# One kernel, four moves: block products in one run with a PSUM tile per bank, weight sums on VectorE, PSUM reads by halves, v over GpSimd's queue

## The chip, the cores and the metric

The kernel runs on one core of a Trainium2 chip. The metric is the device time of one execution in microseconds (us). Three timed runs of the kernel before gave 946.34, 945.3 and 944.76 us, a median of 945.3 us. The profiled execution took 946.52 us; its span, from the first instruction of the program to the last, is 944.7 us.

## What is computed

Attention within chunks of 64 positions (8 batches, 8 heads, 576 positions, head size 64), and then a feed-forward layer with a squared ReLU on the 4608 rows of 512 that it leaves:

```python
scores = scale * np.matmul(q_c, k_c.transpose(0, 1, 2, 4, 3))      # per chunk of 64
scores = scores - np.max(scores, axis=-1, keepdims=True)
attn = np.exp(scores)
attn = attn / (np.sum(attn, axis=-1, keepdims=True) + 1e-09)
out = np.matmul(attn, v_c)
x = out.transpose(0, 2, 1, 3).reshape(B * S, H * D)                # 4608 x 512
h = x @ w_in                                                       # 512 x 2048
g = np.maximum(h, 0.0) ** 2
y = (g @ w_out).astype(np.float32)                                 # 2048 x 512
```

The weights come as float64. Every matrix product of the feed-forward layer is made of three float32r products of a high and a low part (high times high, high times low, low times high).

## The kernel before

Rows are worked on in pairs of chunks, 128 rows each, 36 pairs in all. They form seven blocks: three of 4 pairs ("plain" blocks, numbered 0 to 2) and four of 6 pairs ("mixed" blocks, 3 to 6). The 2048 hidden columns are 16 slices of 128.

In a plain block one slice is 12 matmuls into the bank `h` (L602) and, two slices later, 12 matmuls into four output banks `o` (L638). ReLU, square and the split into high and low part lie between, on ScalarE (ACT) and VectorE (DVE). Block 0 runs beside the conversion of the weights.

In a mixed block two slices are made at once from 7 block products instead of 8, in the manner of Strassen and Winograd. One step is a pair of slices; there are 8 steps in a block and 32 in all. A step has 7 products of 6 matmuls each (L689, 384 columns; P0 to P6 in the order of `WAYS`) and 12 output groups of 3 matmuls each (L721, 512 columns), which multiply the squared columns of the step before by `w_out`. Products go into the one PSUM tile `both` of two banks, side 0 (A) or side 1 (C). P2 and what follows on side 0 adds up on P0, which ACT has first copied aside (`keep`, L695, tile `aside`); DVE adds side 1 and such a copy into `gf` (`add`, L698); the last part goes through ACT's ReLU (`positive`, L701). Then come the square (L704), the high part (ACT, L707) and the low part (DVE, L711). In the order of the work the outputs are spread between the products: the numbers of output groups after P0 to P6 are 0, 1, 0, 1, 2, 0, 0, then 3, then an attention clump, then the rest.

The left factors of the products are sums of blocks of `w_in`. They are made once, during blocks 1 and 2, by GpSimd (POOL): for each of 8 pairs of slices 16 elementwise instructions of 128 by 256 (L749 to L773), a rounding by ACT (L769, tile `combo`, one buffer), and a store of each result to DRAM (L776). The mixed steps fetch them again through a ring of 10 slots (L679). The scratch tile `temp` of the sums lies in the same place as `gf1`, where the first mixed step puts `kept(1)`; the ring, the split right factors `xc` and `gs_f` lie in the places of `w_in` slices, which the sums read. The right factors are built at the start of each mixed block (`build`, L1209, L1211, L1216) from the block's attention output, the tile `aside`.

Attention for pairs 8 to 35 goes in "clumps" between matmuls of the feed-forward layer. A clump is the value products of one pair (`values`, L342, 32 small matmuls) and the scores of the next (`scores`, L296, 32 small matmuls). Both use `both`: scores columns 0 to 255 of either bank, values columns 256 to 511. After the values ACT copies the result out of PSUM (`place`, L353); after the scores DVE reads them twice (`top`, L302; `less`, L306). The softmax, two transposes on DVE and a copy of the transposed probabilities on POOL (`keep_p`, L331), with four small DMAs on SP's queue, make the left factor of the next values. q, k and v come over SP's queue (L240, L270).

The order of the instructions on each engine is written out by a planner (class `Plan`). It has a cost for each operation, names for what is read and written, a rank (lower goes first), a gate, and a slack for attention's matmuls; it emits the instructions in the order of its own clock. The waits on the chip are not the planner's. They follow from which tiles an instruction reads and writes. For the planner the names "A" and "C" stand for the two banks; `scores` and `values` both write them, so that scores come after values by at least the slack of 0.5 us:

```python
entry = min(
    (x for x in ready[e] if max(x[0], free[e]) <= soonest + (hold if x[1] < self.RUSH else 0.0)),
    key=lambda x: (x[1], max(x[0], free[e]), x[2]),
)
```

Of the kernel before, what the change touches and what calls it, by code (L numbers as in the profile page):

```python
# [20 lines left out]
def kernel(  # L21
# [72 lines left out]
    both = psum["at"].tile([P, 2, DM], F32, name="both", tag="both")  # L94
    four = both.rearrange("p c (w h j) -> p c w h j", w=2, j=CH)
# [26 lines left out]
    wi = [None] * NF  # L122
    wo = [None] * NF
# [22 lines left out]
    def convert_w(n):  # L146
# [36 lines left out]
        def high():  # L183
            w = const.tile([P, 2, DM], F32R, name=f"w{kind}{f}", tag=f"w{n}")
            st["w"] = w
            nc.scalar.copy(w[:, 0], st["a"].bitcast(F32))  # L186
            hl = (w[:, 0], w[:, 1])
            if kind == "i":
                wi[f] = tuple(x.rearrange("p (c n) -> p c n", c=NCC) for x in hl)
            else:  # L190
                wo[f] = hl
# [70 lines left out]
    def load_v(pair):  # L262
# [3 lines left out]
        for c in range(2):  # L266
            bb, n0 = divmod(2 * pair + c, NCH)
            for b, r in enumerate(halves):
                s = v[bb, b * HH:(b + 1) * HH, n0 * CH:(n0 + 1) * CH, :]
                nc.sync.dma_start(out=t[r, c], in_=s.rearrange("h j d -> j h d"))  # L270
        return t

    class Quad:
# [19 lines left out]
        def scores(self):  # L293
            for a, t, c, b in itertools.product(range(2), repeat=4):
                h, own, to = 4 * b + 2 * a + t, halves[c], halves[b]
                nc.tensor.matmul(  # L296
                    four[to, c, 0, 2 * a + t], self.t["q"][own, h], self.t["k"][own, h], start=True, stop=True
                )

        def top(self):  # L300
            self.m = att.tile([P, 2, HH, 1], F32, name=f"m{self.pair}", tag="nm", bufs=2)
            nc.vector.tensor_reduce(self.m, four[:, :, 0], axis=AX.X, op=ALU.max)  # L302

        def less(self):
            self.e = late["pool"].tile([P, HH, 2, CH], F32, name=f"e{self.pair}", tag="e")
            nc.vector.tensor_tensor(  # L306
                self.e.rearrange("p h c j -> p c h j"), four[:, :, 0], self.m.broadcast_to([P, 2, HH, CH]),
                op=ALU.subtract,
            )
# [29 lines left out]
        def values(self):  # L339
            for a, c, b, t in itertools.product(range(2), repeat=4):  # L340
                own, to = halves[b], halves[t]
                nc.tensor.matmul(  # L342
                    four[to, b, 1, 2 * a + c], self.v[own, c, 2 * a + t],
# [3 lines left out]
        def place(self, part):  # L347
            j = self.pair - first_pair[self.b]
            got = four[:, :, 1].rearrange("p b (a c) i -> p b a (c i)", c=2)
            if self.b >= NCB:  # L350
                i = j % TH
                to = stage()[:, j // TH, :, i * P:(i + 1) * P].rearrange("p (b a) i -> p b a i", b=2)
                nc.scalar.copy(to, got)  # L353
                return
            xh, xl = (
                x[:, :, j * P:(j + 1) * P].rearrange("p (b a) i -> p b a i", b=2) for x in x_of(self.b)
            )
            if part == 0:
                nc.scalar.copy(xh, got)
            else:  # L360
                nc.vector.tensor_tensor(xl, got, xh.bitcast(F32), op=ALU.subtract)
# [10 lines left out]
    def bank(which, shape, name):  # L372
        kind, n = which
        if kind == "at":
            names = "abcdef"[:len(shape) - 1]
            t = both[:, n, :math.prod(shape[1:])]
# [179 lines left out]
    PARTS = [(q, m) for q in ("b11", "b21", "t1", "t2", "t3", "t4", "b22") for m in range(2)]  # L556
# [12 lines left out]
    def quarter(q):  # L569
# [5 lines left out]
        ("s3", "t3", 0), ("a22", "t4", 0), ("s4", "b22", 1),  # L575
# [94 lines left out]
    class Mixed(Step):  # L670
# [12 lines left out]
        def product(self, i):  # L683
# [3 lines left out]
            for c, u in some:  # L687
                l, r = ((0, 0), (0, 1), (1, 0))[u]
                nc.tensor.matmul(  # L689
                    both[:, side, :HN], w[:, l, c], part(x, r)[:, c], skip_group_check=True,  # L690
# [3 lines left out]
        def keep(self, i):  # L694
            nc.scalar.copy(snap(i), both[:, 0, :HN])  # L695

        def add(self, i, h, s):
            nc.vector.tensor_tensor(kept(i)[:, h * HN:(h + 1) * HN], both[:, 1, :HN], snap(s), op=ALU.add)  # L698

        def positive(self):  # L700
            nc.scalar.activation(kept(1)[:, :HN], both[:, 0, :HN], AF.Relu)  # L701
# [27 lines left out]
    class Combos:  # L729
# [17 lines left out]
        def both_of(self, to, x, y, op):  # L747
            for m in range(2):
                nc.gpsimd.tensor_tensor(self.temp(to + m)[:, 0], self.half(x)[m], self.half(y)[m], op=op)  # L749

        def join(self, to):
            nc.gpsimd.tensor_tensor(
# [3 lines left out]
        def less(self, to, i, x):  # L756
            t = self.temp(i)[:, 0]
            for y in self.half(x):
                nc.gpsimd.tensor_tensor(self.temp(to)[:, 0], t, y, op=ALU.subtract)
                t = self.temp(to)[:, 0]  # L760

        def from_it(self, i, x):
            t = self.temp(i)[:, 0]
            h, l = self.half(x)
            nc.gpsimd.tensor_tensor(t, h, t, op=ALU.subtract)
            nc.gpsimd.tensor_tensor(t, t, l, op=ALU.add)
# [644 lines left out]
```

## Time and profile before

| | |
|---|---|
| median of 3 runs | 945.3 us |
| profiled execution, its own time | 946.52 us |
| its span | 944.7 us |
| PE (matmul) busy | 884.2 us, 94% |
| PEld (weight load) busy | 727.6 us, 77% |
| DVE busy | 523.1 us, 55% |
| ACT busy | 344.6 us, 36% |
| POOL busy | 277.9 us, 29% |

PE's matmuls are pipelined and their ends are modelled, so that a busy PE is not PE at its peak; starts of weight loads (PEld) show its pace better. The number in brackets behind a row of the timeline is the idle time of that engine before the row, and what ended it. An engine other than PE that waits costs nothing as long as PE does not wait for it.

### The profile page before, as it was taken

The numbers are of one execution on the slowest core, as the hardware profiler recorded it, in microseconds if no ns is written. First come the engines' busy times: TensorE is split into PE (matmuls) and PEld (weight loads), VectorE is DVE, ScalarE is ACT, GpSimd is POOL, SyncE is SP. The second block draws the span as 40 slices with busy tenths as digits, with TensorE's granted clock in tenths as the row PEclk, the third lists the DMA queues.
The fourth block names the chain that finished last, engine by engine and source line by source line (L and its number), as shares of the span: only waits on it lengthen the run. The fifth ranks groups of instructions, "written<-read, shape, count | busy, mean of one in ns | idle before, by whom it ended". The sixth has DMA issues, their size and how long they took to land.

```text
span 944.7 us, 16464 instructions
## 1 busy us (share of the span) xinstructions
PE 884.2 (94%) x6142; PEld 727.6 (77%) x6142; DVE 523.1 (55%) x822; ACT 344.6 (36%) x597; POOL 277.9 (29%) x460
## 2 busy tenths in 40 slices
PE   9999999999999853999999999999999999999998
PEld 7787788878888643887778778777787888788886
DVE  6999984334467652445655554566455456332322
ACT  5888864443333322222233322223322224222222
POOL 2000012677667664221222222222212221222200
PEclk9999999999999975999999999999999999999999
DMA  7883534556955452666684677665767642744411
GB/s 193 265 245 112 191 63 111 129 124 151 241 124 127 107 139 68 176 150 143 133 165 129 163 157 155 143 135 116 206 131 155 138 107 78 201 101 113 121 45 68
DMA packets 268384, 132.72 MB, mean 140 GB/s; under 512 B 214416, under 2 KB 229008, under 8 KB 268304
## 3 DMA queue, kind: packets, MB, share of 16 engines
q0 software_dynamic: 43776, 73.42, 30.3%
q1 hardware_dynamic: 222272, 57.59, 27.6%
q8 instruction: 49, 0.80, 0.3%
q10 hardware_dynamic: 2256, 0.66, 0.3%
q14 instruction: 31, 0.25, 0.1%
HBM read 103.81 MB, written 24.12 MB: 135 GB/s over the span
## 4 chain that ended last, share of the span: by engine, by line
PE 54%; DVE 3%; POOL 2%; issue 2%; DMA 2%; ACT 2%; SPq 1%; DVEq 0%; POOLq 0%; ACTq 0%
PE o L721 26%; PE both L689 25%; DVE gf L698 2%; PE both L342 1%; PE both L296 1%; ACT aside L695 1%; DMA combos<-combo 1%; SPq L240 1%; POOL temp L749 1%; POOL combo L773 1%; DMA p<-et 0%; PE o L638 0%; ACT xc L1209 0%; DVE xc L1211 0%; POOL combos L776 0%
## 5 line engine op out<-in xcount | busy, mean ns | idle before, releaser
L689 PE MATMUL both<-xc,ring 128*128 128x384 f32 x1344 | 275.3, 349 | 48.3 <-DVE gf L698 20.2
L689 PEld LDWEIGHTS both<-xc,ring 128*128 128x128 f32 x1344 | 233.6, 191 | 88.9 <-DVE gf L698 39.6
L679 POOL DMA_DIRECT2D ring<-combos x224 | 118.6, 530 | 399.4 <-PE both L689 390.0
L721 PE MATMUL o<-wo,gs_f 128*128 128x512 f32 x576 | 151.9, 393 | 0.0
L721 PE MATMUL o<-wo,gs_s 128*128 128x512 f32 x576 | 148.2, 398 | 0.0
L602 PE MATMUL h<-x,wi 128*128 128x512 f32 x576 | 145.6, 396 | 1.3 <-ACT wi L186 1.0
L638 PE MATMUL o<-wo,gs 128*128 128x512 f32 x576 | 144.0, 395 | 0.0
L698 DVE TENSOR_TENSOR gf<-both,aside 128x384 f32<-128x384 f32 x96 | 53.3, 555 | 160.4 <-ACT aside L695 123.7
L602 PEld LDWEIGHTS h<-x,wi 128*128 128x128 f32 x576 | 105.7, 188 | 26.7 <-DVE wi L195 2.9
L638 PEld LDWEIGHTS o<-wo,gs 128*128 128x128 f32 x576 | 108.4, 190 | 22.4
L721 PEld LDWEIGHTS o<-wo,gs_s 128*128 128x128 f32 x576 | 105.2, 188 | 22.6
L721 PEld LDWEIGHTS o<-wo,gs_f 128*128 128x128 f32 x576 | 106.4, 188 | 14.9
L695 ACT COPY aside<-both 128x384 f32<-128x384 f32 x96 | 46.2, 481 | 193.3 <-PE both L689 193.3
L704 DVE SCALAR_TENSOR_TENSOR gf<-gf 128x768 f32<-128x768 f32 x64 | 61.3, 958 | 82.9 <-ACT gf L701 81.9
L628 DVE TENSOR_TENSOR gs<-g,gs 128x512 fp32r<-128x512 f32 x48 | 38.0, 791 | 59.2 <-ACT gs L625 59.1
L613 ACT ACTIVATE g<-h 128x512 f32<-128x512 f32 x48 | 28.6, 597 | 56.9 <-PE h L602 46.1
L701 ACT ACTIVATE gf<-both 128x384 f32<-128x384 f32 x32 | 15.7, 492 | 88.0 <-PE both L689 86.5
L625 ACT CAST gs<-g 128x512 fp32r<-128x512 f32 x48 | 29.7, 620 | 42.3 <-PE o L638 39.2
L773 POOL TENSOR_TENSOR combo<-temp,combo 128x256 fp32r<-128x256 f32 x32 | 25.1, 783 | 58.2 <-ACT combo L769 58.1
L711 DVE TENSOR_TENSOR gs_s<-gf,gs_s 128x768 fp32r<-128x768 f32 x32 | 29.9, 934 | 21.5 <-ACT gs_s L707 19.7
L312 ACT ACTIVATE e<-e 128x512 f32<-128x512 f32 x28 | 17.7, 632 | 59.8 <-DVE e L306 59.8
L707 ACT CAST gs_f<-gf 128x768 fp32r<-128x768 f32 x32 | 26.7, 836 | 31.7 <-DVE gf L704 31.7
(110 smaller groups left out, 874.0 us busy)
## 6 DMA issues: line engine op xcount, KB each, us to landing
ring<-combos POOLq DMA_DIRECT2D x224, 256.0 KB, 3.3
wiraw<-in_moe_w_in_dram SPq DMA_DIRECT2D x16, 512.0 KB, 5.9
woraw<-in_moe_w_out_dram SPq DMA_DIRECT2D x16, 512.0 KB, 5.4
combos<-combo POOLq DMA_DIRECT2D x32, 256.0 KB, 2.6
out_dram<-ob SPq DMA_DIRECT2D x30, 256.0 KB, 3.3
q_raw<-in_q_dram SPq DMA_DIRECT2D x224, 32.0 KB, 2.3
k_raw<-in_k_dram SPq DMA_DIRECT2D x224, 32.0 KB, 3.1
v_raw<-in_v_dram SPq DMA_DIRECT2D x112, 64.0 KB, 2.6
```

What stands on the lines that cost most here:

```text
L602: nc.tensor.matmul(self.h[:, :self.n], a[:, c], bb[:, c, :self.n], start=c == 0 and i == 0, stop=last,)
L625: nc.scalar.copy(self.gh[:, :self.n], self.g)
L628: nc.vector.tensor_tensor(self.gl[:, :self.n], self.g, self.gh.bitcast(F32)[:, :self.n], op=ALU.subtract)
L638: nc.tensor.matmul(acc[b, j], a[:, j * P:(j + 1) * P], bb, start=f == 0 and i == 0, stop=f == NF - 1 and i == 2,)
L679: nc.gpsimd.dma_start(out=ring(self.m + i).rearrange("p l c n -> p (l c n)"), in_=combos[self.p, i])
L689: nc.tensor.matmul(both[:, side, :HN], w[:, l, c], part(x, r)[:, c], skip_group_check=True, start=(c, u) == (0, 0) and i in (0, 1, 3), sto ...
L695: nc.scalar.copy(snap(i), both[:, 0, :HN])
L698: nc.vector.tensor_tensor(kept(i)[:, h * HN:(h + 1) * HN], both[:, 1, :HN], snap(s), op=ALU.add)
L704: nc.vector.scalar_tensor_tensor(kept(i), kept(i), 0.0, kept(i), op0=ALU.max, op1=ALU.mult)
L711: nc.vector.tensor_tensor(l, kept(i), h.bitcast(F32), op=ALU.subtract)
L721: nc.tensor.matmul(acc[b, j], a[:, j * P:(j + 1) * P], bb, start=first and u == 0, stop=last and u == 2)
L773: nc.gpsimd.tensor_tensor(o[:, 1], self.temp(i)[:, 0], o[:, 0].bitcast(F32), op=ALU.subtract)
```

## The change

- The tile `both` becomes two tiles `sides`, one for each bank. Everything that read both banks in one instruction now has two: `top`, `less` and `place`.
- The order of the products becomes P0 to P4 as before, then `s4`/`b22` and `a22`/`t4`, so that the two sides alternate from first to last. All seven run without output groups between them, except in the very first mixed step, with four groups after P1. One more copy aside (`keep(0, 1)`) takes the place of a direct read, since the last product on side 0 now carries ReLU.
- The evictions of the products get the planner's rank -20, and a rule by which ACT and DVE are held free up to 0.95 us for them.
- For the planner, each bank has two halves: scores write A0 and C0, values write A1 and C1, products write all four. Scores no longer follow values by these names.
- Weight sums: all elementwise instructions move from POOL to DVE; `both_of` becomes one instruction of 512 columns instead of two of 256. They begin at slice 18 instead of 21.
- `keep_p` moves from POOL to ACT, the v loads from SP's queue to POOL's, and the squares of block 2 from DVE to ACT. The last attention clump before the mixed blocks moves from 1.8 to 1.0 slices ahead of the end.

```diff
-    both = psum["at"].tile([P, 2, DM], F32, name="both", tag="both")
-    four = both.rearrange("p c (w h j) -> p c w h j", w=2, j=CH)
+    sides = [psum["at"].tile([P, DM], F32, name=f"side{n}", tag=f"at{n}") for n in range(2)]
+    four = [t.rearrange("p (w h j) -> p w h j", w=2, j=CH) for t in sides]
...
-                nc.sync.dma_start(out=t[r, c], in_=s.rearrange("h j d -> j h d"))
+                nc.gpsimd.dma_start(out=t[r, c], in_=s.rearrange("h j d -> j h d"))
...
-            nc.vector.tensor_reduce(self.m, four[:, :, 0], axis=AX.X, op=ALU.max)
+            for c in range(2):
+                nc.vector.tensor_reduce(self.m[:, c], four[c][:, 0], axis=AX.X, op=ALU.max)
...
-            nc.gpsimd.tensor_copy(self.p, self.et)
+            nc.scalar.copy(self.p, self.et)
...
+            for b in range(2):
+                got = four[b][:, 1].rearrange("p (a c) i -> p a (c i)", c=2)
+                own = slice(2 * b, 2 * b + 2)
+                if self.b >= NCB:
+                    i = j % TH
+                    nc.scalar.copy(stage()[:, j // TH, own, i * P:(i + 1) * P], got)
+                    continue
...
-        ("s3", "t3", 0), ("a22", "t4", 0), ("s4", "b22", 1),
+        ("s3", "t3", 0), ("s4", "b22", 1), ("a22", "t4", 0),
...
-            for m in range(2):
-                nc.gpsimd.tensor_tensor(self.temp(to + m)[:, 0], self.half(x)[m], self.half(y)[m], op=op)
+            nc.vector.tensor_tensor(self.temp(to, 2), a, b, op=op)
...
-            nc.gpsimd.tensor_tensor(o[:, 1], self.temp(i)[:, 0], o[:, 0].bitcast(F32), op=ALU.subtract)
+            nc.vector.tensor_tensor(o[:, 1], self.temp(i)[:, 0], o[:, 0].bitcast(F32), op=ALU.subtract)
...
+        KEPT = -15
+        KEEP = 0.95
...
+                def wait(x):
+                    return (self.KEEP if x[1] < self.KEPT else hold if x[1] < self.RUSH else 0.0) if hold else 0.0
...
-            dve = s.b > 1
+            dve = s.b == 2 < NCB - 1 or s.b > 2
...
-            add(PE, 0.6, x.scores, ["qt", "kt"], ["sc", "A", "C"] + [("at", n) for n in range(2) if pair == NN],
+            add(PE, 0.6, x.scores, ["qt", "kt"], ["sc", "A0", "C0"] + [("at", n) for n in range(2) if pair == NN],
...
             elif n == 4:
-                add(ACT, 0.5, lambda: s.keep(0), ["A"], ["s0"])
-                add(DVE, 0.56, lambda: s.add(1, 1, 0), ["C", "s0"], [("kept", 1, 1)] + temp)
+                add(DVE, 0.56, lambda: s.add(1, 1, 0, 0), A + ["s0"], [("kept", 1, 1)] + temp)
             elif n == 5:
-                add(ACT, 0.5, lambda: s.positive(), ["A"], [("kept", 1, 0)] + temp)
-                square_of(s, 1)
+                add(DVE, 0.56, lambda: s.add(0, 1, 1, 1), C + ["s1"], [("kept", 0, 1)])
             elif n == 6:
-                add(DVE, 0.56, lambda: s.add(0, 1, 1), ["C", "s1"], [("kept", 0, 1)])
+                add(ACT, 0.5, lambda: s.positive(), A, [("kept", 1, 0)] + temp)
+                square_of(s, 1)
                 square_of(s, 0)
...
-                when.append(ends - NF + 0.3 + j * (NF - 2.1) / (SB - 1))
+                when.append(ends - NF + 0.3 + j * (NF - 1.3) / (SB - 1))
...
-        mix_at = [NF + 5 + (ends - NF - 9) * c / NFP for c in range(NFP)]
+        mix_at = [NF + 2 + (ends - NF - 9) * c / NFP for c in range(NFP)]
...
-                for i, more in enumerate((0, 1, 0, 1, 2, 0, 0)):
+                for i, more in enumerate((0, 4 if s.m == 0 else 0, 0, 0, 0, 0, 0)):
```

## Rows read from the trace of the kernel before

**Rows 1.** Waits of weight loads, 375 to 945 us: total, times, longest.

```profile
PEld both L689 <- DVE gf L698: 38.6, 62, 1.4
PEld both L689 <- ACT aside L695: 14.5, 47, 0.3
```

**Rows 2.** Timeline, step without attention: start, length, what [idle before].

```profile
865.69 2.17 PEld L689 LDWEIGHTS both<-xc,ring 128*128 128x128 f32 x12
867.85 0.59 PEld L721 LDWEIGHTS o<-wo,gs_f 128*128 128x128 f32 x3
868.22 0.48 ACT L695 COPY aside<-both 128x384 f32<-128x384 f32 x1 [1.49 <-PE both L689]
868.73 0.56 DVE L698 TENSOR_TENSOR gf<-both,aside 128x384 f32<-128x384 f32 x1 [1.02 <-ACT aside L695]
869.34 2.06 PEld L689 LDWEIGHTS both<-xc,ring 128*128 128x128 f32 x12 [0.90 <-DVE gf L698]
...
878.15 4.06 PEld L721 LDWEIGHTS o<-wo,gs_s 128*128 128x128 f32 x18
882.25 2.17 PEld L689 LDWEIGHTS both<-xc,ring 128*128 128x128 f32 x12
```

**Rows 3.** Timeline, an attention clump and the whole step after it.

```profile
464.44 0.56 PEld L342 LDWEIGHTS both<-p,v_raw 64*64 64x64 f32 x32 [0.35 <-issue]
465.07 0.53 PEld L721 LDWEIGHTS o<-wo,gs_s 128*128 128x128 f32 x3
465.21 0.59 ACT L353 COPY aside<-both 128x512 f32<-128x512 f32 x1 [1.01 <-PE both L342]
465.96 0.56 PEld L296 LDWEIGHTS both<-kt,qt 64*64 64x64 f32 x32 [0.36 <-ACT aside L353]
...
468.89 2.06 PEld L689 LDWEIGHTS both<-xc,ring 128*128 128x128 f32 x12 [0.38 <-DVE e L306]
...
487.59 2.04 PEld L689 LDWEIGHTS both<-xc,ring 128*128 128x128 f32 x12 [0.23 <-DVE e L306]
```

**Rows 4.** Timeline, the two steps around the start of block 5.

```profile
634.54 2.03 PEld L689 LDWEIGHTS both<-xc,ring 128*128 128x128 f32 x12 [0.23 <-DVE e L306]
...
669.37 2.03 PEld L689 LDWEIGHTS both<-xc,ring 128*128 128x128 f32 x12 [1.11 <-issue]
```

**Rows 5.** Timeline, from the last plain slice to the second mixed step.

```profile
325.20 0.22 PEld L342 LDWEIGHTS both<-p,v_raw 64*64 64x64 f32 x4 [1.71 <-POOL temp L749]
332.39 3.70 PEld L689 LDWEIGHTS both<-xc,ring 128*128 128x128 f32 x12 [3.34 <-DVE e L306]
343.78 3.22 PEld L689 LDWEIGHTS both<-xc,ring 128*128 128x128 f32 x11 [5.74 <-DVE xc L1211]
367.76 0.56 DVE L698 TENSOR_TENSOR gf<-both,aside 128x384 f32<-128x384 f32 x1 [17.89 <-POOL combo L773]
368.89 1.78 PEld L689 LDWEIGHTS both<-xc,ring 128*128 128x128 f32 x6 [17.55 <-ACT gf L701]
374.96 2.15 PEld L689 LDWEIGHTS both<-xc,ring 128*128 128x128 f32 x12
```

**Rows 6.** Busy time by engine in that stretch, then PE's granted clock.

```profile
325.00:375.00 50.00, 21.95 (x130) 18.95 (x131) 20.60 (x25) 12.40 (x23) 28.85 (x43) 0.62 0.41 103
```

**Rows 7.** Timeline, rounding of the first and low part of the last of 32 sums.

```profile
162.48 0.39 ACT L769 CAST combo<-temp 128x256 fp32r<-128x256 f32 x1
...
367.00 0.72 POOL L773 TENSOR_TENSOR combo<-temp,combo 128x256 fp32r<-128x256 f32 x1 [0.51 <-ACT combo L769]
```

**Rows 8.** DMA issues: out<-in, queue, count, KB each, median us to landing.

```profile
combos<-combo POOLq DMA_DIRECT2D x32, 256.0 KB, 2.6
```

**Rows 9.** Groups of instructions: count, busy us, mean ns.

```profile
L1211 DVE TENSOR_TENSOR xc<-aside,xc 128x768 fp32r<-128x768 f32 x28 | 26.7, 974 | 7.3 <-ACT xc L1209 5.1 <-POOL temp L749 2.1
L650 ACT COPY aside<-o 128x256 f32<-128x256 f32 x2 | 0.6, 375 | 0.8 <-PE o L721 0.8
```

More of the change, by code (lines that the diff above doesn't have):

```diff
@@ L122 @@
     wi = [None] * NF
+    whole = [None] * NF
     wo = [None] * NF
@@ L296, in scores @@
                 nc.tensor.matmul(
-                    four[to, c, 0, 2 * a + t], self.t["q"][own, h], self.t["k"][own, h], start=True, stop=True
+                    four[c][to, 0, 2 * a + t], self.t["q"][own, h], self.t["k"][own, h], start=True, stop=True
                 )
@@ L342, in values @@
                 nc.tensor.matmul(
-                    four[to, b, 1, 2 * a + c], self.v[own, c, 2 * a + t],
+                    four[b][to, 1, 2 * a + c], self.v[own, c, 2 * a + t],
                     self.p[own, 2 * a + t, c].rearrange("p n i -> p (n i)"), start=True, stop=True,
@@ L348, in place @@
             j = self.pair - first_pair[self.b]
[L349 to L361, printed above, removed]
+            for b in range(2):
[5 more added lines that the diff above has]
+                    continue
+                xh, xl = (x[:, own, j * P:(j + 1) * P] for x in x_of(self.b))
+                if part == 0:
+                    nc.scalar.copy(xh, got)
+                else:
+                    nc.vector.tensor_tensor(xl, got, xh.bitcast(F32), op=ALU.subtract)
     def x_of(b):
@@ L894, in run, with best @@
                 hold = self.HOLD.get(e, 0.0)
-                entry = min(
-                    (x for x in ready[e] if max(x[0], free[e]) <= soonest + (hold if x[1] < self.RUSH else 0.0)),
-                    key=lambda x: (x[1], max(x[0], free[e]), x[2]),
-                )
+                def best(some):
+                    return min(some, key=lambda x: (x[1], max(x[0], free[e]), x[2]))
+                def wait(x):
+                    return (self.KEEP if x[1] < self.KEPT else hold if x[1] < self.RUSH else 0.0) if hold else 0.0
+                entry = best(x for x in ready[e] if max(x[0], free[e]) <= soonest + wait(x))
+                until = max(entry[0], free[e])
+                if until > soonest and entry[1] < self.KEPT:
+                    short = [x for x in ready[e] if max(x[0], free[e]) + ops[x[2]][1] <= until + 0.05]
+                    if short:
+                        entry = best(short)
                 t, _, n = entry
@@ L1087, in load_quad @@
                         size=P * DM, line=("raw", nm))
-            add(SP, 4 * ISSUE, x.load_values, [], [("a", pair % VBUFS)], size=P * DM * 4)
+            add(POOL, 4 * ISSUE, x.load_values, [], [("a", pair % VBUFS)], size=P * DM * 4)
             p.rank += 1
@@ L1104, in scores @@
             add(DVE, 0.73, x.turn_p, [("e", i)], ["et"])
-            add(POOL, 1.1, x.keep_p, ["et"], [("p", i)] + [("p", i, *y) for y in itertools.product(range(2), repeat=2)])
+            add(ACT, ONE, x.keep_p, ["et"], [("p", i)] + [("p", i, *y) for y in itertools.product(range(2), repeat=2)])
             for b, m in itertools.product(range(2), repeat=2):
@@ L1110, in values @@
             x = quads[pair]
-            add(PE, 0.6, x.values, [("a", pair % VBUFS), ("p", pair % 2)] + [("p", pair % 2, *y) for y in itertools.product(range(2), repeat=2)], ["xt", "A", "C"], slack=SLACK, gate=gate)
+            add(PE, 0.6, x.values, [("a", pair % VBUFS), ("p", pair % 2)] + [("p", pair % 2, *y) for y in itertools.product(range(2), repeat=2)], ["xt", "A1", "C1"], slack=SLACK, gate=gate)
             if x.b >= NCB:
@@ L1279, in parts_of @@
                 if first:
-                    old = wide(NF - 2 + m) if i else [("g" + y, m) for y in "hl"]
+                    old = wide(NF - 2) + wide(NF - 1) if i else [("g" + y, n) for y in "hl" for n in range(2)]
                 add(e, cost, lambda fn=fn: fn(i), g + [("sg", i, 0)] * m, [("sg", i, m)] + old)
@@ L1340, in program @@
         p.rank = LASTS
-        some = [(lambda s=s, j=j: out_group(s, j), None) for s in ffn[-LAG:] for j in range(blocks[s.b])]
+        some = [(lambda s=s, j=j: out_group(s, j), 0) for s in ffn[-LAG:] for j in range(blocks[s.b])]
         for b in range(NCB, len(blocks)):
```

71 lines of the change are left out of this document (40 added, 31 removed).

## The prediction

> **What bounds the kernel now.** I read the busy times by engine first: matmuls 94% of the span, so the sum is made on TensorE's (PE) path, and a gain can only come from time in which PE waits. Since the ends of matmuls are modelled, I read the waits of the weight loads next, in the mixed blocks [rows 1]: two lines carry them, both at the products (L689), on DVE's `add` (38.6 us, 62 times) and on ACT's `keep` (14.5 us, 47 times). Then the timeline of one step without attention [rows 2], from one P0 to the next: 882.25 - 865.69 = 16.57 us. P2 writes side 0, whose only reader, `keep`, ends at 868.70; yet it starts at 869.34, just behind an `add` that reads side 1 and ends at 869.29. And `keep`, which reads what P0 wrote, starts at 868.22, when P1 is through. So the two banks are ordered as one tile, and one output group does not cover two reads in a row: 0.90 us idle.
>
> Last, I read the stretch from the last plain slice to the second mixed step [rows 5, 6]. It has 49.76 us (325.20 to 374.96), with PE busy for 21.95 of 50 and a granted clock of 0.62, so partly at the lower level, 1.2 GHz: behind 3.34 us of idle time 12 weight loads take 3.70 us, against 2.06 elsewhere [rows 2]. The long waits are 3.34 (DVE's `less`), 5.74 (split factors) and 17.55 us (ReLU). Behind the last stands `add` on DVE, which waited 17.89 us for POOL's last weight sum: `temp` and `gf1` share a place.
>
> **A, the passage into the mixed blocks.** The work of PE in it is 42 products at 2.06/12 = 0.172 us (7.2), 24 output matmuls at 0.228 (18 take 882.25 - 878.15 = 4.10; 5.5 in all) and a clump (2.3, below): 15.0 us. To it come stalls that remain.
> - Weight sums. Today 32 results take 162.48 to 367.00, 6.4 us each [rows 7]. They begin three slices earlier, some 16 us. A result needs the rounding (0.39), the low part (0.72 on POOL now), an issue and a landing (2.6) [rows 7, 8]: some 4.5 with hops, so near 1.9 us of the 6.4 is waiting for engines. A DVE instruction of this width has no row; a third of a 768-wide one, as the width goes, and all of it [rows 9] bound it by 0.32 and 0.97 us, and I take 0.42, nearer the third. With that and one engine less crowded I take 6.0 us each, so the end falls near 162 - 16 + 31 x 6.0 = 332; at 5.2 it is 307, at 6.4 it is 344. The first mixed step needs `temp` behind P4, some 8 us after P0. So the 17.55 and 5.74 us go; I leave 1 us (0 to 8).
> - What is late next is DVE's chain for the right factors: four subtractions and five low parts at 0.974 [rows 9], 8.8 us in a row, and of a better rank than `less` of the clump, for which P0 waits. The 3.34 us stays and can grow; I take 5 us (3 to 7), since seven groups of plain work (4.8 us) now stand between clump and P0.
> - The clock. A wait of 5 us may lower it again; the work behind it at half pace costs 0 to 5 us; I take 4.
>
> Together 15 + 10 = 25, against 49.8: a gain of 24.8 us (stalls of 3 to 18 us give 32 to 17).
>
> **B, the other 31 steps.** Without waits a step is 42 x 0.172 + 36 x 0.228 + 0.1 = 15.5 us. With a tile per bank, each of P2 to P6 waits only for the read of its own side, and one product lies between. That product covers 1.03 us. The read starts 0.37 us after the next run's first weight load (868.22 - 867.85), takes 0.48 or 0.56, and the load follows 0.05 after its end [rows 2]: 0.90 for `keep`, 0.98 for `add`. Both fit, with 0.13 and 0.05 us to spare, so I take 15.6 and, for the range, 0.1 us late at each of five reads, 16.1.
> - 7 steps without attention or block start: 7 x (16.57 - 15.6) = 6.8.
> - Three block starts, two steps each: 669.37 - 634.54 = 34.83 [rows 4], of which 1.11 is the wait of the next P0 for `add`, the last read today; afterwards `positive` is last on side 0, with outputs to cover it. 2 x 15.6 + 0.3 for factors that come late: a gain of 3.3 each, 10.
> - 18 steps with a clump: 487.59 - 468.89 = 18.70 today [rows 3]. Here the change gives something back. Today the planner puts an output group (465.07) between values and scores, and still the scores wait 0.36 us for `place`, which reads columns that scores do not write. With the new names scores have no edge to values, the same rank and are ready, so they come directly behind them. `place` starts 0.21 us after the last weight load of the values; it is two instructions of 0.375 [rows 9] instead of one of 0.59; the scores follow 0.16 us behind (465.96 - 465.80). That is a bare wait of 1.12 us. The clump costs 0.35 + 0.56 + 1.12 + 0.56 + 0.07 = 2.7, the step 18.3: a gain of 0.4, 18 times, 8.
>
> Sum 24.8 us (28 with 15.5; 9 with 16.1).
>
> **C, plain blocks.** Nine clumps more than the one in A pay for the same order without the gain: 1.52 - 0.68 = 0.84 us between values and scores today (the output group taken off), 0.56 + 1.12 = 1.68 then. A loss of 9 x 0.84 = 7.6 us (5.4 to 9).
>
> Whether a read of half a bank holds back a write to the other half is not shown by rows 3 alone, since today's read spans both banks. The Trainium skill, "PSUM — Partial Sum Buffer", section "PSUM bank collisions raise a hardware error", says to guard by bank and quadrant, not by address. By that rule the scores wait, as in the sum above; by columns alone, the 28 waits of 1.12 us would not be there.
>
> **At nothing.** v's four loads go on POOL's queue behind the values that free their buffer; ring fetches behind them have three products of lead, and the next values come 18.7 us later [rows 3]. `keep_p` on ACT and the second halves of `top` and `less` (0.2 us each) lie under nine output groups. DVE gets some 6 us per pair of slices and ACT the squares of block 2 where PE has a full slice of 5.5 us to cover them. Were that cover gone, a plain slice would lengthen by what is late, under 1 us.
>
> **The sum.** -24.8 - 24.8 + 7.6 = -42 us. The profiled execution took 946.5 us; 904.5 follows, and with the median 1.2 us below the profiled one, 903.3.
>
> **Rivals.**
> 1. *Halves do not conflict.* 28 x 1.12 = 31 us less: 872. For it: the new names say that its writer counted on it. Against: whole banks are ordered as one today. Chance 0.07.
> 2. *The sums stay late.* Their chain may be set by landings, not by POOL: at 6.9 us each they end near 360, and the first step stalls 15 us more: 918. For it: 2.6 us of landing stays in every result. Chance 0.10.
> 3. *Slower: reads late in the run of products.* DVE and ACT finish what they have begun; an instruction of 0.97 us [rows 9] in front of a read costs half of it, 0.48, on average, at five reads in each of 31 steps: +74 us, 977. It decides from 42/155 = 0.27 us a read. For it: only 0.05 us to spare behind `add`, and no output group as cover. Against: the hold of 0.95 us for just these reads. Chance 0.07.
> 4. *The two tiles are still ordered as one.* Then each product waits for the read of the one before it, some 0.92 us bare, 155 times: 1046. Chance 0.02.
>
> **How the numbers follow.** The forecast has 0.72; 0.02 is left for a change too small to tell from none (0.2%, 1.9 us, is about what a measurement of this kernel can tell). The ends of the terms give 946.5 - 1.2 - (32 + 28 - 5.4) = 891 and 945.3 - (17 + 9 - 9) = 928; all ends at once are unlikely, so 890 to 926, which takes in rival 2 and leaves out 1, 3 and 4. Faster: 0.72 + 0.07 + 0.10 = 0.89; within 0.2%: 0.02; slower: 0.09.
>
> **What would show it.** Right: no wait of L689 on `add` or `keep` over 0.1 us in the timeline of a step; P0 to P0 near 15.6 us late in the run; scores directly behind values with near 1.1 us idle, released by ACT's L353 successor; the last weight sum before 345 us; the passage near 25 us. Wrong: idle time inside the seven products (rivals 3 and 4), no idle time between values and scores (rival 1), a long wait for ReLU in the first mixed step (rival 2), or plain slices over 5.5 us.

## The result, and the profile after

The changed kernel takes 905.4 us (median; 904.9 to 905.7), the kernel before 945.8 us (944.8 to 947.6): a ratio of 0.957, 95% interval 0.9554 to 0.9587. The forecast was 903.3. The total is near it, but its terms are not: the passage into the mixed blocks gained next to nothing, and the rest gained what the passage did not. The profiled execution has a span of 903.5 us, 41.2 less than before. Cut at the weight loads of the first product of each step (P0), on both traces:

| stretch | before, us | after, us | gain, us |
|---|---|---|---|
| start to the first P0 | 332.4 | 319.9 | 12.5 |
| first mixed step, P0 to P0 | 42.6 | 46.9 | -4.3 |
| 18 steps with an attention clump | 336.0 | 319.5 | 16.6 |
| three block starts, two steps each | 104.8 | 95.4 | 9.3 |
| 7 last steps, with the tail | 128.9 | 121.8 | 7.2 |

The waits of the weight loads from 300 to 910 us come first (engine, tile, line, releaser: total, times, longest). They answer to [rows 1]; the lines of the products have moved to L691, of `add` to L700, of `keep` to L697.

```profile
PEld side L691 <- DVE gf L700: 19.8, 17, 1.6
PEld side L691 <- issue: 15.5, 1, 15.5
PEld side L691 <- DVE xc L1227: 13.7, 2, 12.8
```

`keep` is gone as a releaser, and `add` holds a product back 17 times in place of 62. Two long waits stand alone. Which steps have the 17, two timelines show (start, length, what, [idle before]). A step without attention, which answers to [rows 2]:

```profile
797.25 7.38 PEld L691 LDWEIGHTS side<-xc,ring 128*128 128x128 f32 x42
798.73 0.48 ACT L697 COPY aside<-side 128x384 f32<-128x384 f32 x1 [0.45 <-PE side L691]
...
812.76 7.38 PEld L691 LDWEIGHTS side<-xc,ring 128*128 128x128 f32 x42
```

All 42 weight loads of the seven products run in one go of 7.38 us, and the step is 812.76 - 797.25 = 15.51 us (before 16.57). `keep`, which reads P0, starts 1.5 us behind the first weight load, when P1 cannot be through: 12 loads take 2.1 us. A step whose forerunner held a clump, and the clump behind it, which answers to [rows 3]:

```profile
419.63 3.21 PEld L691 LDWEIGHTS side<-xc,ring 128*128 128x128 f32 x18
420.16 0.62 ACT L334 COPY p<-et 128x512 f32<-128x512 f32 x1 [2.65 <-DVE et L328]
421.12 0.48 ACT L697 COPY aside<-side 128x384 f32<-128x384 f32 x1 [0.33 <-PE side L691]
421.49 0.84 ACT L709 CAST gs_s<-gf 128x768 fp32r<-128x768 f32 x1
422.36 0.96 DVE L713 TENSOR_TENSOR gs_s<-gf,gs_s 128x768 fp32r<-128x768 f32 x1 [2.23 <-ACT gs_s L709]
423.42 0.56 DVE L700 TENSOR_TENSOR gf<-side,aside 128x384 f32<-128x384 f32 x1
424.03 4.13 PEld L691 LDWEIGHTS side<-xc,ring 128*128 128x128 f32 x24 [1.19 <-DVE gf L700]
...
430.51 0.56 PEld L345 LDWEIGHTS side<-p,v_raw 64*64 64x64 f32 x32 [0.37 <-issue]
430.97 0.56 PEld L298 LDWEIGHTS side<-kt,qt 64*64 64x64 f32 x32
...
431.71 0.65 ACT L357 COPY aside<-side 128x256 f32<-128x256 f32 x2 [2.68 <-PE side L298]
```

Read from the end. The scores (L298) follow the values (L345) without a wait, 0.46 us from start to start against 1.52 in [rows 3]; `place` (L357) runs behind the scores, and by its releaser it waited for them. The 1.12 us that I had put between the two isn't there. In its place the fourth product (424.03) waits 1.19 us for `add`, which stood in DVE's queue behind a remainder (L713), which waited for a rounding (L709), which stood in ScalarE's (ACT's) queue behind the copy of p (L334), which waited 2.65 us for DVE's transposition. That copy is the one that the change took from GpSimd (POOL).

Last the passage, which answers to [rows 5], and its granted clock, which answers to [rows 6] (busy us and count of PE, PEld, DVE, ACT, POOL; then clock, DMA share, GB/s):

```profile
314.16 0.56 PEld L345 LDWEIGHTS side<-p,v_raw 64*64 64x64 f32 x32 [0.35 <-issue]
...
315.25 1.92 PEld L604 LDWEIGHTS h<-x,wi 128*128 128x128 f32 x9
317.21 2.68 PEld L640 LDWEIGHTS o<-wo,gs 128*128 128x128 f32 x12
319.93 2.17 PEld L691 LDWEIGHTS side<-xc,ring 128*128 128x128 f32 x12
...
337.83 5.03 PEld L691 LDWEIGHTS side<-xc,ring 128*128 128x128 f32 x17 [12.85 <-DVE xc L1227]
...
360.34 1.78 PEld L691 LDWEIGHTS side<-xc,ring 128*128 128x128 f32 x6 [15.49 <-issue]
...
366.80 7.38 PEld L691 LDWEIGHTS side<-xc,ring 128*128 128x128 f32 x42
```

```profile
314.00:367.00 53.00, 24.77 (x153) 21.16 (x152) 30.12 (x54) 14.74 (x30) 11.14 (x20) 0.71 0.39 103
```

From the values to the second P0 it has 366.80 - 314.16 = 52.64 us, where before had 49.76 and I had forecast 25. The two stretches don't hold the same work. In the kernel before the last plain work stood ahead of these values (325.20 in [rows 5]), with only attention between them and P0:

```profile
320.81 2.68 PEld L638 LDWEIGHTS o<-wo,gs 128*128 128x128 f32 x12
...
328.11 0.94 PEld L296 LDWEIGHTS both<-kt,qt 64*64 64x64 f32 x32 [0.86 <-ACT aside L353]
```

After the change 21 matmuls of the plain work, 319.93 - 315.25 = 4.68 us, stand behind them. On the same work the passage takes 48.0 us, 1.8 less than before. What it waits for are the weight sums (the list of their tile, then the timeline at its end):

```profile
L774 ACT CAST combo<-temp x32: 390/401/419, 143.8 to 358.8; 128x256 fp32r<-128x256 f32 x32
...
  DMA combos<-combo: 16.6, 5
```

```profile
336.09 0.69 DVE L754 TENSOR_TENSOR temp<-wi,wi 128x512 f32<-128x512 f32 x1
336.82 0.83 ACT L1225 CAST xc<-aside 128x768 fp32r<-128x768 f32 x1 [1.22 <-DVE temp L754]
336.82 1.83 DVE L1227 TENSOR_TENSOR xc<-aside,xc 128x768 fp32r<-128x768 f32 x2
...
351.74 0.40 ACT L774 CAST combo<-temp 128x256 fp32r<-128x256 f32 x1 [3.42 <-DMA combos<-combo]
...
355.25 0.40 ACT L774 CAST combo<-temp 128x256 fp32r<-128x256 f32 x1 [3.11 <-DMA combos<-combo]
...
359.21 0.42 DVE L778 TENSOR_TENSOR combo<-temp,combo 128x256 fp32r<-128x256 f32 x1 [1.91 <-ACT combo L774]
359.66 0.56 DVE L700 TENSOR_TENSOR gf<-side,aside 128x384 f32<-128x384 f32 x1
```

The first rounding is 18.7 us sooner than in [rows 7] (143.8 against 162.5), the last remainder only 7.8 us (359.2 against 367.0): (358.8 - 143.8)/31 = 6.94 us for each result, where before, with its last rounding at 366.5, had 6.58. With nothing else left to run a result takes 355.25 - 351.74 = 3.51 us, and over the whole stretch only five instructions waited for a store to land, 16.6 us in all, every one of them behind 331 us. So neither the landing nor the arithmetic sets the 6.94 us. At the end `add` (359.66) stands right behind the last remainder, as in [rows 5], and the product behind it starts at 360.34.

### The profile page after: what moved, and what is told of

Its sections match the earlier page's. It is cut to its first block, busy times and chain, and to the rows that moved or that the text cites. A ratio compares the mean times of both kernels' runs of the same rounds, so it can differ in the third digit from the quotient of the medians.

```text
span 903.5 us, 16529 instructions
## 1 busy us (share of the span) xinstructions
PE 852.5 (94%) x6142; PEld 732.0 (81%) x6142; DVE 548.3 (61%) x962; ACT 369.4 (41%) x669; POOL 242.4 (27%) x432
## 4 chain that ended last, share of the span: by engine, by line
PE 79%; DVE 8%; issue 4%; DMA 3%; ACT 2%; SPq 2%; POOL 1%; DVEq 0%; POOLq 0%; ACTq 0%
PE o L723 30%; PE side L691 22%; PE o L640 12%; PE h L604 12%; PE side L345 2%; DVE gs_s L713 2%; PE side L298 2%; ACT gs_s L709 1%; SPq L260 1%; DVE gf L700 1%; ACT aside L697 1%; DMA k_raw<-in_k_dram 1%; DMA woraw<-in_moe_w_out_dram 1%; DVE woa L175 1%; DVE wia L175 1%
## 5 line engine op out<-in xcount | busy, mean ns | idle before, releaser
L691 PE MATMUL side<-xc,ring 128*128 128x384 f32 x1344 | 248.7, 340 | 42.6 <-DVE gf L700 29.5
L691 PEld LDWEIGHTS side<-xc,ring 128*128 128x128 f32 x1344 | 237.5, 190 | 51.7 <-DVE gf L700 19.8
L723 PE MATMUL o<-wo,gs_f 128*128 128x512 f32 x576 | 142.3, 395 | 0.0
L723 PE MATMUL o<-wo,gs_s 128*128 128x512 f32 x576 | 135.9, 389 | 0.0
L700 DVE TENSOR_TENSOR gf<-side,aside 128x384 f32<-128x384 f32 x96 | 53.5, 558 | 103.7 <-PE side L691 101.5
L272 POOL DMA_DIRECT2D v_raw<-in_v_dram x112 | 69.8, 636 | 93.6 <-PE side L345 68.9
L697 ACT COPY aside<-side 128x384 f32<-128x384 f32 x96 | 46.0, 479 | 93.8 <-PE side L691 93.4
L713 DVE TENSOR_TENSOR gs_s<-gf,gs_s 128x768 fp32r<-128x768 f32 x32 | 30.6, 957 | 64.5 <-ACT gs_s L709 64.5
L703 ACT ACTIVATE gf<-side 128x384 f32<-128x384 f32 x32 | 15.7, 492 | 78.4 <-PE side L691 78.4
L713 DVE TENSOR_TENSOR gs_f<-gf,gs_f 128x768 fp32r<-128x768 f32 x32 | 30.0, 936 | 28.0 <-ACT gs_f L709 28.0
L305 DVE TENSOR_REDUCE m<-side 128x4 f32<-128x256 f32 x56 | 21.1, 419 | 39.9 <-ACT aside L357 36.9
```

What stands on the lines that cost most here:

```text
L272: nc.gpsimd.dma_start(out=t[r, c], in_=s.rearrange("h j d -> j h d"))
L691: nc.tensor.matmul(sides[side][:, :HN], w[:, l, c], part(x, r)[:, c], skip_group_check=True, start=(c, u) == (0, 0) and i in (0, 1, 3), st ...
L697: nc.scalar.copy(snap(i), sides[side][:, :HN])
L700: nc.vector.tensor_tensor(kept(i)[:, h * HN:(h + 1) * HN], sides[side][:, :HN], snap(s), op=ALU.add)
L713: nc.vector.tensor_tensor(l, kept(i), h.bitcast(F32), op=ALU.subtract)
L723: nc.tensor.matmul(acc[b, j], a[:, j * P:(j + 1) * P], bb, start=first and u == 0, stop=last and u == 2)
```

## The experiments

Three theories were open. *Copy:* the wait in the clump steps comes from the place of p's copy in ScalarE's queue. *Order:* the sums are late because the planner places them late, not because of their engine or their landing. *Bank:* accesses to one tile keep the order of the program, whatever columns they touch, and the tile per bank carries the gain in the steps. All kernels start from the changed one unless said otherwise. The kernel before ran beside each group, with medians of 945.4 to 946.1 us.

**1. p's copy back on GpSimd**, in the planner's list too (at 1.1 us).

```diff
-            nc.scalar.copy(self.p, self.et)
+            nc.gpsimd.tensor_copy(self.p, self.et)
```

> The one edit: attention's copy of p from et (28 of them) goes back from ScalarE to GpSimd; all else as in the changed kernel. Theory: in the 17 steps that hold an attention clump ScalarE's queue has this copy ahead of the step's first rounding; it waits there for VectorE's transposition, so rounding, remainder and the sum add(0, 0) come late and the fourth product waits 1.19 us for it. Without it that wait is gone: 17 x 1.19 = 20 us less, some 885 us (880 to 890), clump steps of 16.8 in place of 18.0 us. Rival A: the wait has another cause beside it (the remainder on VectorE, which stands behind attention's softmax in VectorE's own queue), and goes on: 903 to 907. Rival B: the copy by GpSimd ends later, values wait for p, and what the fourth product gains is lost at the next clump: 895 to 905.

885.6 us (ratio to before 0.9357, 0.9341 to 0.9372). The clump steps take 16.83 us in place of 18.0, and the products run through (timeline of one):

```profile
400.19 7.38 PEld L691 LDWEIGHTS side<-xc,ring 128*128 128x128 f32 x42
400.39 0.83 ACT L709 CAST gs_s<-gf 128x768 fp32r<-128x768 f32 x1 [2.31 <-PE o L723]
400.82 0.62 POOL L334 COPY p<-et 128x512 f32<-128x512 f32 x1 [4.24 <-DVE et L328]
```

The copy still waits for the transposition (until 400.82), but on an engine where nothing urgent stands behind it; the rounding starts at 400.39, while the copy is still waiting. This part of the change cost 19.8 us, as the copy theory said. Both of its rivals are out.

**2. The weight sums early in the order.**

```diff
-                    p.rank = 5000
+                    p.rank = 900
-                add(POOL, 1.0, lambda: c.store(name), ["ch", "cl"], [("combo", c.p, side_of[name])], size=P * DM * 4)
+                add(POOL, 0.3, lambda: c.store(name), ["ch", "cl"], [("combo", c.p, side_of[name])], size=P * DM)
```

> The edit is of the order alone: the weight sums rank ahead of attention's clumps (900 in place of 5000), and the planner counts a store of a sum at 0.3 us with a quarter of the bytes in place of 1.0 us with all; the instructions are the same ones. Theory: the sums end late because of their place in the order, not because of what they cost; with their last rounding ahead of the first product (before 320 us of the span) the waits of 12.9 and 15.5 us in the passage go, and with them most of the half clock there: 905.4 - 28 - 2 = 875 us (868 to 882). Rival A: the sums go by the landing of each store (about 2.5 us and the next rounding behind it) and by VectorE's share of the plain steps, so that early places only put ScalarE's queue in front of a landing and take from the plain steps what the passage gives: 895 to 910. Rival B: the splits of the first block need those 30 us themselves, so the waits shrink to half: 888 to 893.

872.1 us (0.9221, 0.9207 to 0.9234), 33.3 less than the changed kernel. The last rounding comes at 313.0 us, ahead of the first product, (313.0 - 143.8)/31 = 5.46 us for each; the first mixed step takes 14.5 in place of 46.9 us (the list of the sums' tile, then the timeline):

```profile
L774 ACT CAST combo<-temp x32: 397/406/418, 143.8 to 313.0; 128x256 fp32r<-128x256 f32 x32
```

```profile
320.27 2.17 PEld L691 LDWEIGHTS side<-xc,ring 128*128 128x128 f32 x12
...
325.14 4.54 PEld L691 LDWEIGHTS side<-xc,ring 128*128 128x128 f32 x25
331.23 0.82 PEld L691 LDWEIGHTS side<-xc,ring 128*128 128x128 f32 x5 [1.55 <-DVE xc L1227]
...
334.75 2.35 PEld L691 LDWEIGHTS side<-xc,ring 128*128 128x128 f32 x13
```

The 28.3 us of the two long waits are down to 1.55, and the splits need none of that time. The half clock goes with the waits: from 314 to 335 us the granted clock is 1.00, the higher level (2.4 GHz), in place of 0.71; 25 weight loads take 4.54 us, 0.18 each, where behind 12.85 us of idle time 17 took 5.03, 0.30 each. The plain steps lost nothing. The order theory holds.

**3. One half of that edit.** The store counted cheaper, the rank left at 5000.

> From the changed kernel, one half of the edit that put the sums early: the planner counts a store of a sum at 0.3 us and a quarter of the bytes, while the sums keep their rank behind attention's clumps. Theory: the planner's price of a store set the pace of the sums (6.9 us each); with it low the last rounding comes some 25 us sooner (before 335 us of the span) and most of the gain is there without the rank: 874 to 882 us. Rival: the rank is what holds the sums back, and this alone moves the last rounding by under 10 us: 893 to 905 us.

879.2 us (0.9294, 0.928 to 0.9309). The last rounding comes at 333.8, (333.8 - 144.8)/31 = 6.10 us each, and the first mixed step takes 21.1 us. So 26 of the 33 us hang on the planner's price for a store. The rank, on top of it, brings the other 7.

**4. The sums' engine.** Additions and remainders back on GpSimd, at the costs that the planner had for them before.

> The edit: the weight sums' additions and remainders go back from VectorE to GpSimd, with the costs that the planner had for them before, and start at the same slice as in the changed kernel. Theory: a sum's pace is that of its place in the order, not of the engine; the last rounding comes within 10 us of where it stood (358.8 us of the span), and the time within 8 us of the changed kernel's, 897 to 913 us. Rival: VectorE's shorter additions (0.42 against some 0.66 us by GpSimd, for half of a weight) are what let the first rounding and the last one come earlier, and without them the last one falls back by 8 us or more: 913 to 922 us.

902.4 us (0.9539, 0.9525 to 0.9553), 3 us *less* than by VectorE, though a remainder takes 0.74 us there against 0.42. The last rounding is at 356.7 in place of 358.8 us, the first mixed step 44.3 in place of 46.9. The move to VectorE brought nothing.

**5. The sums' start.** The kernel of 4 with the start back where it was before, three slices later.

> From the changed kernel: the weight sums by GpSimd, as in the kernel with that one edit (902.4 us), and their start put back by three slices of the plain stage to where it was before. Theory: what the changed kernel's passage did gain over the one before came from the earlier start alone; the last rounding falls back from 356.7 us of the span by 10 to 17 us, and the time goes to 912 to 920 us. Rival: the first rounding comes later, but the last one stays, since the order's places near the passage are free anyway: 900 to 905 us.

917.4 us (0.9698, 0.9683 to 0.9712): the last rounding falls back by 15.7 to 372.4 us, the first mixed step takes 59.1 us. So of all that was done to the sums the earlier start alone paid, 15.0 us. With the engine and the start of the kernel before, the last rounding still comes 5.9 us later than there (372.4 against 366.5): some other part of the change puts the sums back, and no run shows which.

**6. One tile over both banks.**

```diff
-    sides = [psum["at"].tile([P, DM], F32, name=f"side{n}", tag=f"at{n}") for n in range(2)]
+    both = psum["at"].tile([P, 2, DM], F32, name="both", tag="both")
+    sides = [both[:, n] for n in range(2)]
```

> The one edit: the two PSUM tiles are again two views of one tile that covers both banks; the single run of products, the reads by halves and all else stay. Theory: accesses to one tile are kept in program order even where they lie in different banks, so each of the seven products waits for the read of the product before it, on the other bank; by the prediction's fourth rival that is 1,046 us (1,020 to 1,070), with six waits of 0.6 to 0.9 us in every one of the 32 product steps. Rival: what orders them is the bank itself (the addresses that overlap), and one tile over two banks costs nothing: 903 to 908 us.

1,030.6 us (1.0901, 1.0881 to 1.0922). A step without attention (lines are one higher in this kernel):

```profile
957.54 2.17 PEld L692 LDWEIGHTS both<-xc,ring 128*128 128x128 f32 x12
957.76 2.27 PE L692 MATMUL both<-xc,ring 128*128 128x384 f32 x12
960.07 0.48 ACT L698 COPY aside<-both 128x384 f32<-128x384 f32 x1 [1.50 <-PE both L692]
960.60 1.00 PEld L692 LDWEIGHTS both<-xc,ring 128*128 128x128 f32 x6 [0.89 <-ACT aside L698]
960.60 1.32 PE L692 MATMUL both<-xc,ring 128*128 128x384 f32 x6 [0.57 <-ACT aside L698]
962.01 0.56 DVE L701 TENSOR_TENSOR gf<-both,aside 128x384 f32<-128x384 f32 x1 [2.45 <-PE both L692]
962.62 1.01 PEld L692 LDWEIGHTS both<-xc,ring 128*128 128x128 f32 x6 [1.03 <-DVE gf L701]
...
977.61 2.17 PEld L692 LDWEIGHTS both<-xc,ring 128*128 128x128 f32 x12
```

`keep` (960.07) reads what P0 left on side 0, and starts when P1, on side 1, is through (957.76 + 2.27 = 960.03, by the modelled end). `add` (962.01) reads side 1, and starts when P2, on side 0, is through (960.60 + 1.32 = 961.92). The next product into the bank that was read then waits for this late read: P2 for `keep`, P3 (962.62) for `add`. So the theory had the link wrong (a product that waits for a read of the *other* bank); here the read waits for the other bank, and the product for the read of its own. What it said of the order is right. Five such waits of 0.89 to 1.04 us (not six) make the step 20.07 us against 15.5. The bank theory holds, and the rival by addresses is out.

**7. The products spread again**, with a tile per bank: between them none, one, none, one, two, none, none output groups, as before.

> The edit: the seven products no longer run in one go; from the second step on, groups of output products stand between them again as in the kernel before (none, one, none, one, two, none, none), while the PSUM tiles stay one per bank. Theory: with a tile per bank the single run gives nothing by itself, since no product waits in a plain step either way, and the spread order covers the late sum add(0, 0) of the clump steps: 17 x 0.6 to 17 x 1.2 = 10 to 20 us less in the clump steps, 885 to 896 us. Rival: fewer changes between products and output groups are what makes a plain step 15.5 in place of 16.6 us, and spread they cost up to 0.5 us each over 31 steps: 910 to 921 us.

893.8 us (0.9448, 0.9434 to 0.9462). A plain step takes 15.62 us against 15.53 in one run, so the run itself is worth 0.1 us a step; a clump step takes 16.94 against 18.0, since an output group lies where the fourth product waited.

**8. One tile and spread.** The edits of 6 and 7 together.

> One tile over both banks, and the products spread among the output groups as in the kernel before (none, one, none, one, two, none, none); all else as in the changed kernel. Theory: the spread order was the remedy for the one tile: the output groups stand where a product would have waited for a read on the other bank. So this is a long way under the single run on one tile, and the difference to the spread order with a tile per bank (893.8) is what the tile per bank is worth in that order: 31 steps at 0.6 to 1.2 us, 912 to 931 us. Rival: the spread order hides all of it, and the tile per bank is worth nothing unless the products run in one go: 892 to 896.

953.2 us (1.0093, 1.0064 to 1.0122), 59 us over the spread order with a tile per bank, and more than either theory gave. A plain step fits (16.86 against 15.62, 1.24 more); a clump step loses 19.3 - 16.94 = 2.4 us. In one of these (446 to 455 us) the third product waits 1.43 us for an `add` that stands behind attention's softmax on VectorE (0.90 in a plain step), and the fifth 1.21 us for a `keep` behind p's copy on ScalarE (0.69 in a plain step): reads of the other bank that come late count too (here, unlike in 6, the product does wait for the other bank), and I had priced them all as in a plain step. The tile per bank is the part of the change that carries the steps, in either order.

**9. v's loads back on SP's queue.**

> The one edit: the loads of v go back from GpSimd's queue to SP's (28 pairs, four transfers each). Theory: no transfer of v was late before or after, and SP has room, so the time stays within 0.4%: 902 to 909 us. Rival: on SP the four transfers of v stand ahead of the moves of p, which then land late for the values' products: some 0.5 us for each of the 28 clumps, 912 to 920 us.

907.1 us (0.9596, 0.958 to 0.9612): beside the 905.4 this is 1.7 us, and the two intervals overlap. The profiled execution has lost 2.9 us by the second P0 (369.7 against 366.8 us), where the length hangs on the sums, and 0.3 behind it; the clump steps are the same 18.0. The queue of v makes no difference in the steps.

**10. Both edits that paid**, 1 and 2 together.

> Both edits that paid alone: p's copy back on GpSimd, and the weight sums early in the order. Theory: the two lie in different stretches (the clump steps after 335 us, the passage before it) and add: 885.6 - (45.4 - 14.5 us of the first product step) = 854.7, so 852 to 858 us. Rival: with the sums early GpSimd's queue has their stores ahead of p's copies in the plain steps, values wait there, and 5 to 15 us of the sum are lost: 860 to 870.

853.6 us (0.9033, 0.902 to 0.9047). The two add (905.4 less 19.8 and 33.3 is 852.3), and this beats both kernels. The waits of its weight loads from 130 us on, and its busy times in the passage and behind it:

```profile
PEld side L345 <- issue: 10.1, 28, 0.4
PEld side L691 <- DVE xc L1227: 1.5, 1, 1.5
...
```

```profile
314.00:336.00 22.00, 20.71 (x159) 17.89 (x158) 18.41 (x30) 11.23 (x21) 7.56 (x13) 1.00 0.52 119
336.00:840.00 504.00, 504.00 (x3538) 452.59 (x3537) 287.51 (x446) 153.47 (x270) 162.38 (x288) 1.00 0.62 150
```

From 336 to 840 us the records show PE without a gap (by its modelled ends), at a granted clock of 1.00. The only idle time of the weight loads that is left there is the 0.37 us ahead of the values of each clump, 18 times, 6.6 us, for which the profile shows no releaser.

**11. Values, then `place`, then scores.** From the kernel of 10, the planner's names for the two halves of a bank are joined again:

```diff
-            add(PE, 0.6, x.scores, ["qt", "kt"], ["sc", "A0", "C0"] + [("at", n) for n in range(2) if pair == NN],
+            add(PE, 0.6, x.scores, ["qt", "kt"], ["sc", "A", "C"] + [("at", n) for n in range(2) if pair == NN],
-            A, C = ["A0", "A1"], ["C0", "C1"]
+            A, C = ["A"], ["C"]
```

and likewise where values (`"A1", "C1"`) and products write.

> From the kernel with both edits (853.6 us): the planner's names for the two halves of each bank are joined again, as in the kernel before, so that in the order of the program one group of matmuls and the reads of the values' half (place) come between the values' products and the scores, which in the changed kernel follow on the values directly. Theory: reads of a bank and later writes to its other half are kept in program order, so the scores now wait for the second read of place: 0.3 us (a group of output matmuls covers most of it) to 1.1 us (none of it) in each of 27 clumps, 862 to 883 us, with PE waits at the scores released by ScalarE. Rival: two halves of one bank don't wait for each other, and what is new is only where a group stands: 852 to 857 us, no such wait.

874.3 us (0.9244, 0.9229 to 0.926), 20.8 more. A clump:

```profile
527.94 0.56 PEld L345 LDWEIGHTS side<-p,v_raw 64*64 64x64 f32 x32 [0.36 <-issue]
528.57 0.53 PEld L723 LDWEIGHTS o<-wo,gs_f 128*128 128x128 f32 x3
528.67 0.65 ACT L357 COPY aside<-side 128x256 f32<-128x256 f32 x2 [2.21 <-PE side L345]
529.46 0.56 PEld L298 LDWEIGHTS side<-kt,qt 64*64 64x64 f32 x32 [0.36 <-ACT aside L357]
```

Here `place` reads each bank by itself, in columns that the scores don't write, and the scores wait for it all the same, though an output group lies between: values to scores 1.52 us again. So accesses to one tile hold each other back even in two halves of its bank; what decides who waits is which comes first in the program. These waits, like those of 6, are asked for by the program, by the tiles that its instructions read and write; whether the chip could do without them no run here shows. The Trainium skill's rule that I had cited ("PSUM — Partial Sum Buffer", section "PSUM bank collisions raise a hardware error": guard by bank and quadrant) agrees with this row as to the order; the error itself no run here shows. Of the 20.8 us not all is this wait: the steps of the later blocks take 17.23 us, 0.40 more each, but the first six lose 14 us, where products now also wait for `less` (five times, 7.3 us). In these six the values stand 3.9 to 4.1 us ahead of the next P0, and `less` ends 4.2 to 4.3 us behind them; in the later blocks they stand 7.5 us ahead of it. Why the order puts the six so late, I didn't settle.

## Why the prediction was right or wrong

**The waits inside the products: right.** A plain step was to be 15.6 us and is 15.5; the seven steps gave 7.2 us (6.8 forecast), the block starts 9.3 (10). That the two banks had been ordered as one tile, read from [rows 2], is borne out by 6 and 8. Rival 4 was priced at 1,046 us; built, it takes 1,031, at 0.9 to 1.0 us for five products of a step, though by another link than the one that I gave (6). What the rank of the evictions and the hold of 0.95 us for them are worth, no run shows.

**A, the passage: wrong, by 23 us.** It was to gain 24.8 and gained 1.8 on the same work. (From the values on it lost 2.9, 49.8 to 52.6; my 25 us had left out the 4.8 us of plain work that I myself put behind the clump.) The step that failed is the pace of the sums, 6.0 us each, derived from [rows 7, 8] by taking "1.9 us of the 6.4" as waiting for engines. (From the first of 32 results to the last there are 31 intervals, so it was 6.6.) It was waiting for a place in the order. The pace stayed at 6.94 us, rival 2's figure with another cause: with another order of the same instructions, and stores that land no faster (2.6 us against 2.5), the pace was 5.46 us. So the end came at 359 and not at 332. The instruction itself was sized right (0.42 us). Also wrong in A was what comes next: P0 does not wait for `less`, and VectorE's chain of splits, for which I had left 5 us, held the third product for 12.85 us, since the place that a split writes was still to be read by a late sum (L754 at 336.09, and the rounding L1225 that by its releaser waited for it). The clock was forecast at 4 us; the two waits and the half clock in them cost 46.9 - 14.5 = 32.4 us together. Two slips carry nothing: the longest stalls add up to 20 us, not 18, and the sums of a pair of slices are 14 elementwise instructions in the trace before (112 for the eight pairs), not 16.

**C, the plain clumps, and the 1.12 us in B: wrong, by the order.** I foresaw that scores come directly behind values, and put `place` between them all the same. That the scores come first turns the wait round: `place` waits for the scores, off PE's path. In place of 7.6 us lost, the stretch up to the passage's values gained 325.20 - 314.16 - 4.68 = 6.4 us on the same work: nine clumps at 0.36 (3.3), 1.4 from the wait before the values in [rows 5] (1.71, of which 0.35 is still there), and 1.9 from before 134 us. For rival 1 the mechanism is wrong (11) and its gain came all the same: from 130 us on the scores wait three times, 1.1 us in all.

**At nothing, p's copy: wrong, 20 us.** I named nine output groups on PE as its cover. They hide the copy's own 0.62 us; they don't hide what stands behind it in ScalarE's queue while it waits 2.65 us for VectorE. This is rival 3, at one read in each clump step and 1.19 us a time, where I had looked for long instructions in front of a read and not for waiting ones. The step was forecast at 18.3 with 1.12 us for the scores and is 18.0 with 1.19 for the copy: nearly the same number from another cause. The 18 steps gained 16.6 us (8 forecast).

**The total: right by luck, by errors that cancel.** Up to the second P0 I forecast a gain of 24.8 - 7.6 = 17.2 us and it was 12.5 - 4.3 = 8.2; behind it I forecast 24.8 and it was 33.0. 42.0 against 41.2 us. Of the signs of being wrong that I had named, the long wait in the first mixed step (rival 2), the missing idle time between values and scores (rival 1) and, in the clump steps, idle time inside the seven products (rivals 3 and 4) all showed.

## What to carry to other kernels

Before an instruction that waits is moved to another engine, list what stands behind it in that engine's queue: its own length may be hidden while its wait is not (0.62 us moved, 19.8 us lost). When a chain of small work has a slower pace than its parts by themselves (6.94 us against 3.51), look at where the order puts it before a faster engine is given to it. A total that comes out right shows little; cut both spans where the same work lies between the cuts, and compare term by term.

## What was not expected of the hardware

The sums by GpSimd, with 0.74 us for a remainder against VectorE's 0.42, ended 2.1 us sooner than by VectorE and the kernel was 3 us faster. On one tile over two banks a read of one bank starts when the matmuls into the other that stand ahead of it are through, and the next product into the bank that was read comes 0.89 to 1.04 us late, 4.5 us a step. Reads and writes of one tile wait for each other in program order even where their columns are disjoint, so whether that costs PE anything (0.36 us a clump or nothing) hangs on which comes first. Both are waits that the program asks for; what the chip would do without them no run shows.
